# One sum of all experts in 32 slot columns, and the first block's rows from four partial sums

## The chip, the core and the metric

The kernel runs on one core of a Trainium2 chip. The metric is the device time of one execution in microseconds. Before the change its median over three runs is 196.35 us (196.34 to 196.45).

A core has these engines, each with its own instruction queue, worked off in order: TensorE (PE; its weight loads are shown apart as PEld), VectorE (DVE), ScalarE (ACT) and GpSimd (POOL). SyncE (SP) issues transfers here, and POOL issues those of the weights. Sixteen transfer engines move the data. SBUF holds 128 partitions; TensorE writes into PSUM, eight banks, from which VectorE and ScalarE copy results out. In a matmul one operand is loaded as weights (rows x columns) and the other streams through.

## What is computed

A gated recurrence runs over 4 sequences of 5056 tokens with 256 channels, and its output goes through a mixture of experts with 32 slots (8 experts with 4 slots each):

```python
f = lower_bound + (1 - lower_bound) * sigmoid(f_logit);  i = 1 - f
h[t] = f[t] * h[t-1] + i[t] * x[t]                 # per sequence and channel
logits = h @ phi                                   # 20224 x 32
d = softmax of logits over all tokens              # per slot
slot_input = d.T @ h                               # 32 x 256
slot_out[e] = relu(slot_input[e] @ w1[e]) @ w2[e]  # 8 experts, F = 1024
c = softmax of logits over the 32 slots            # per token
out = c @ slot_out                                 # 20224 x 256, f32
```

Every output row needs all of `slot_out`, and `slot_out` needs every token. So nothing of the output can leave before the experts are done.

## The kernel before

**First phase.** Groups of 512 tokens are loaded, gated, turned to channels, scanned by VectorE, turned back, and fed to the logits and to the slot sums. The exponentials of the logits stay in `etall` (bf16): 32 partitions for each of the four sequences, one column for each token. The weights come in by POOL's queue (`load_w`, L135): `w1` for eight experts, then `w2` for eight. The last two experts' `w2` lie in `w_t`, and the last of all is loaded in two issues, 6 and 2 of its 8 pieces (L144). All orders are written out by hand (`manual_schedule`), so each engine takes its work in the order of the code.

**Experts.** The slot inputs go through `w1`, four experts at a time (L661), and the rectified hidden values are transposed by TensorE (L674). The first four experts then use `hid`: for every expert and piece a weight block of 32 slot columns in which only the expert's own four are not zero. Piece `fc` works on column group `fc % 4`, so four groups of 32 PSUM partitions each hold a partial sum (L693). It is copied out as `so4` (L699). The other four experts use `wide`: the same columns repeated four times, once for each sequence, so 128 columns (L707). Between them one f32 matmul with `rep2`, a 128x128 pattern of 32x32 identities, adds the four partial sums of `so4` and repeats them (L711). So `so_ps` holds the complete `slot_out` four times, one below the other. Row sums of the weights (L413), a long f32 matmul without use for the result (`long_spin`, L156) and two more (`spin`, L152) stand between the experts.

**From slots to rows.** `slot_out` is cast to bf16 (L720). POOL multiplies it by two parity columns into `slot_bd` (L722), so that one matmul with 64 rows serves two sequences at once.

**Output.** `pieces` (L765) makes the first block of sequence 0, 16 rows for each partition, in steps of 2, 2, 2, 4 and 6 rows. Each row is a matmul of 32 partitions of `etall` with `slot_out` (`share`, L736), then ScalarE (first half of a step) and VectorE (second half) scale it by `rrow` into `ob_first`, and SP issues a transfer for each step (L777). Then `by_rows` (L780) makes the last, shorter block, two sequences at a time from `slot_bd` (L788), scaled by VectorE and ScalarE in turn (L730, L795) into `oc`, and sent by two transfers (L753). Then come `rest`, the other three sequences of the first block (`whole`, L808), and the middle block (`couple`, L819). The first stage takes its PSUM tiles by `first_op` from two banks of `psu` and six of `pfirst`.

Of the kernel before, what the change touches and what calls it, by code (L numbers as in the profile page):

```python
# [9 lines left out]
F32 = mybir.dt.float32  # L10
BF16 = mybir.dt.bfloat16
# [7 lines left out]
def kernel(  # L19
# [148 lines left out]
    with tc.tile_pool(name="sp2", bufs=3) as sp2, \  # L168
# [332 lines left out]
        for n in range(n_unit):  # L501
# [94 lines left out]
            elif not n >= n_unit - 6:  # L596
# [2 lines left out]
                batch(slots, n - 4, 1)  # L599
                if n > 2 * B and n % (2 * B) == 3:  # L600
                    idle(1)
        hid, wide = (ld.tile([P, 2, R, D], F32, name=i, tag="x_t") for i in ("hid", "wide"))
        hid = hid.rearrange("p u r d -> p (u r d)").bitcast(BF16)[:, ds(0, FC * E // 2 * NS)]
        wide = wide.rearrange("p u r d -> p (u r d)").bitcast(BF16)[:, ds(0, FC * E // 2 * P)]
        nc.gpsimd.memset(hid, 0.0)
        nc.gpsimd.memset(wide, 0.0)
        hid = hid.rearrange("p (f e s) -> p f e s", f=FC, s=NS)
        wide = wide.rearrange("p (f w b s) -> p f w b s", f=FC, b=B, s=NS)
        logits(last, [3])
        late_exps()  # L610
        left_over()
# [24 lines left out]
    ofirst = ctx.enter_context(tc.tile_pool(name="ofirst", bufs=1, side="right"))  # L636
    ob_first = ofirst.tile([P, wide_r * D + 120], F32, name="ob_first")
    ob_first = ob_first[:, ds(0, wide_r * D)].rearrange("p (r d) -> p r d", d=D)

    with tc.tile_pool(name="ew", bufs=1) as ew, \  # L640
         tc.tile_pool(name="pm", bufs=2, space=PSUM) as pm, \
         tc.tile_pool(name="pbig", bufs=1, space=PSUM) as pbig:

        rep2 = rep.rearrange("p b s -> p (b s)")

        sin = ew.tile([P, DC, NS], BF16, name="sin")
        for o in range(DC):
            nc.vector.scalar_tensor_tensor(sin[:, o], sin_ps[:, o], omlb[:, ds(o, 1)], rcs,
                                           ALU.mult, ALU.mult)

        Q = 4
        H = F // 2
        his = []
        for q in range(E // Q):
            hi = ew.tile([P, F], BF16, name=f"hi{q}")
            for k in range(2):
                hi_ps = (psu.tile([P, H], F32, name="hi_ps", tag="up") if q == 0 else
                         pbig.tile([P, H], F32, name="hi_ps", tag=f"hi_ps{k}"))
                for o in range(DC):
                    for j in range(Q):  # L660
                        nc.tensor.matmul(hi_ps[ds(j * NS, NS)], sin[:, o],  # L661
                                         w1_sb[q * Q + j][:, o, ds(k * H, H)],
                                         start=(o == 0), stop=(o == DC - 1),
                                         skip_group_check=True)
                if k == 0:
                    nc.scalar.activation(hi[:, ds(k * H, H)], hi_ps, ACT.Relu)
                else:
                    nc.vector.tensor_scalar_max(hi[:, ds(k * H, H)], hi_ps, 0.0)
            his.append(hi)
        for q in range(E // Q):  # L670
            ht_ps = psu.tile([P, FC, P], BF16, name="ht_ps", tag="up")
            hi_v = his[q].rearrange("p (c f) -> p f c", f=FC)
            for fc in range(FC):
                nc.tensor.transpose(ht_ps[:, fc], hi_v[:, fc], ident)  # L674
            if q == 0:
                src = ht_ps.rearrange("p f (j s) -> p f j s", s=NS)[:, :, :, ds(0, SPE)]
                src = bass.AP(tensor=src.tensor, offset=src.offset,
                              ap=[list(src.ap[0]), [P, FC], [NS + SPE, Q], [1, SPE]])
                dst = hid[:, :, :, ds(0, SPE)]
                dst = bass.AP(tensor=dst.tensor, offset=dst.offset,  # L680
                              ap=[list(dst.ap[0]), [Q * NS, FC], [NS + SPE, Q], [1, SPE]])
                nc.scalar.copy(dst, src)
                continue
            for j in range(Q):
                s0 = (Q + j) * SPE
                src = ht_ps[:, :, ds(j * NS + s0, SPE)]
                copy = nc.scalar.copy if j % 2 == 0 else nc.vector.tensor_copy
                copy(wide[:, :, j, :, ds(s0, SPE)],
                     src.unsqueeze(2).broadcast_to([P, FC, B, SPE]))
        so4_ps = pm.tile([P, D], F32, name="so4_ps", tag="pm")  # L690
        for e in range(Q):
            for fc in range(FC):
                nc.tensor.matmul(so4_ps[ds(fc % 4 * NS, NS), :], hid[:, fc, e],  # L693
                                 w2_sb[e][:, fc],
                                 start=(e == 0 and fc < 4),
                                 stop=(e == Q - 1 and fc >= FC - 4),
                                 skip_group_check=True)
        so4 = ew.tile([P, D], F32, name="so4")
        nc.vector.tensor_copy(so4, so4_ps)  # L699
        so_ps = pm.tile([P, D], F32, name="so_ps", tag="pm")  # L700
        row_sums(1, range(4, 16))
        nc.vector.reciprocal(rrow[:, :wide_r], rs_ps[:, :wide_r])
        for j in range(Q):
            if j == 2:
                long_spin(tail[:, 1], 3)
            for fc in range(FC):
                nc.tensor.matmul(so_ps, wide[:, fc, j].rearrange("p b s -> p (b s)"),  # L707
                                 w2_sb[Q + j][:, fc], start=j == 0 and fc == 0,
                                 stop=j == Q - 1 and fc == FC - 1, skip_group_check=True)
            if j == 0:  # L710
                nc.tensor.matmul(so_ps, rep2, so4, start=False, stop=False,  # L711
                                 skip_group_check=True)
                row_sums(2)
            if j == 1:
                q = n_grp * R - 1
                nc.vector.reciprocal(rrow[:, wide_r:q], rs_ps[:, wide_r:q])
                nc.vector.reciprocal(rrow[:, q, ds(0, B // 2)], rs_ps[:, q, ds(0, B // 2)])
        ops = [psu.tile([P, 2, D], F32, name="op", tag="up")]
        spin(ops[0].rearrange("p u d -> p (u d)"), 2, G)
        nc.vector.tensor_copy(slot_out, so_ps)  # L720
        for u in range(2):
            nc.gpsimd.tensor_scalar_mul(slot_bd[:, u], slot_out, parity[:, ds(u, 1)])  # L722


    held.close()
# [1 line left out]
    with tc.tile_pool(name="osb", bufs=3) as osb:  # L727
# [37 lines left out]
        def pieces(i, b):  # L765
            dst = rows_of(i, b)
            ob = ob_first
            r0 = 0
            for k in (1, 1, 1, 2, 3):
                for j in range(2):  # L770
                    for r in range(r0 + j * k, r0 + j * k + k, 2):
                        n = min(2, r0 + j * k + k - r)
                        op = first_op()
                        share(op, i, b, r, n)
                        (by_scalar, by_vector)[j](ob[:, ds(r, n)], op[:, ds(0, n)],
                                                  scale_of(i, b, r, n))
                nc.sync.dma_start(out=dst[:, ds(r0, 2 * k)], in_=ob[:, ds(r0, 2 * k)])  # L777
                r0 += 2 * k

        def by_rows(i, j):  # L780
            t0, n_r = blocks[i]
# [119 lines left out]
```

## Time and profile before

| | |
|---|---|
| median of three runs | 196.35 us |
| the profiled execution's own time | 196.46 us |
| its span on the core | 194.7 us |
| PE busy | 148.0 us (76%) |
| VectorE busy | 142.1 us (73%) |
| ScalarE busy | 138.4 us (71%) |
| POOL busy | 102.5 us (53%) |
| read from HBM, written to it | 58.23 MB, 20.71 MB |

The span is the time between the first and the last instruction that the profiler recorded; all positions below are microseconds from its start. A row of a view of instructions reads: start, length, engine, line of the code, operation, output tile <- input tiles, shape; a group has its number of instructions behind an x, and its length is that from the first's start to the last's end. In brackets stand the idle time of the engine before it and what ended that. A window's row has for each engine its busy time and the number of instructions, then the clock that TensorE was granted (1.00 is full), the share of the transfer engines that was busy, and GB/s. "DMA to landing" is the time from the start of an issue until the data are in place.

### The profile page before, as it was taken

What the parts mean: (1) busy time and instruction counts of PE and PEld (TensorE: products, weight loads), DVE (VectorE), ACT (ScalarE), POOL (GpSimd) and SP (SyncE); (2) the same over time, 40 slices, a digit from 0 to 9 for tenths busy, and PEclk for the clock granted to TensorE, in tenths of its full rate; (3) what the DMA queues carried; (4) which work ended last, traced back from release to release, by engine and by line L of the source; (5) the groups of instructions that cost most, each with busy time, mean ns of one, the idle gap of its engine ahead of it and who ended that gap; (6) DMA issues with size and microseconds to landing.
All of it is one profiled execution on the core that took longest, in us unless ns stands there. A gap on an engine that the chain in (4) does not pass through costs nothing.

```text
span 194.7 us, 3260 instructions
## 1 busy us (share of the span) xinstructions
PE 148.0 (76%) x1216; PEld 105.2 (54%) x1216; DVE 142.1 (73%) x176; ACT 138.4 (71%) x192; POOL 102.5 (53%) x77
## 2 busy tenths in 40 slices
PE   0685686997989979898898976999696999980000
PEld 0474555685767758666685765667461764420000
DVE  2666899899799999999999999443178767770000
ACT  3687889799789998899998697421068688992000
POOL 2586877874998688884979977580030000000000
PEclk9999999699999999999999999999996555555555
DMA  5999999999999999999999999999939999999995
GB/s 200 418 434 423 428 428 421 431 431 356 373 426 426 405 338 423 426 428 344 391 412 398 269 221 213 214 215 214 177 149 425 432 447 431 431 431 431 431 431 222
DMA packets 11953, 70.75 MB, mean 363 GB/s; under 512 B 1297, under 2 KB 1682, under 8 KB 7458
## 3 DMA queue, kind: packets, MB, share of 16 engines
q1 hardware_dynamic: 9456, 62.13, 76.4%
q0 software_dynamic: 2480, 8.42, 21.6%
q8 instruction: 9, 0.15, 0.3%
q14 instruction: 6, 0.05, 0.1%
q10 hardware_dynamic: 2, 0.00, 0.0%
HBM read 58.23 MB, written 20.71 MB: 406 GB/s over the span
## 4 chain that ended last, share of the span: by engine, by line
PE 31%; DVE 23%; DMA 19%; ACT 6%; POOL 6%; issue 4%; SPq 1%; POOLq 1%; ACTq 0%; DVEq 0%
DVE h L334 16%; DMA w_t<-in_moe_w_dram 10%; PE op L829 7%; DMA w_sb<-in_moe_w_dram 6%; PE op L740 5%; POOL u_t L247 5%; PE hp L347 4%; PE up L266 4%; PE sp L251 4%; DMA f_t<-in_f_logit_dram 4%; DVE ht L366 3%; ACT s_t L236 3%; DVE oc L730 2%; PE lg L380 2%; PE slot_ps L185 1%
## 5 line engine op out<-in xcount | busy, mean ns | idle before, releaser
L247 POOL TENSOR_TENSOR u_t<-s_t,x_t 128x1024 bf16<-128x1024 bf16 (+1 forms) x39 | 82.3, 2127 | 21.7 <-ACT s_t L236 14.8
L334 DVE TENSOR_TENSOR_SCAN h<-a,h,up 128x512 bf16<-128x512 f32 x64 | 78.1, 1266 | 5.5 <-PE up L266 2.8
L236 ACT ACTIVATE s_t<-f_t 128x2048 bf16<-128x2048 f32 (+2 forms) x23 | 38.2, 1669 | 5.9 <-DMA f_t<-in_f_logit_dram 5.7
L347 PE MATMUL hp<-ident_f,h 128*128 128x128 f32 (+1 forms) x160 | 29.1, 305 | 7.4 <-DVE ht L366 4.7
L347 PEld LDWEIGHTS hp<-ident_f,h 128*128 128x128 f32 (+1 forms) x160 | 23.1, 206 | 16.4 <-DVE ht L366 9.3
L299 ACT ACTIVATE a<-sp,lbs 128x1024 f32<-128x1024 bf16 x28 | 29.7, 1114 | 2.2 <-PE sp L251 2.2
L251 PE MATMUL sp<-ident_f,s_t 128*128 128x128 f32 x144 | 21.4, 292 | 7.1 <-ACT s_t L236 5.7
L266 PE MATMUL up<-ident_f,u_t 64*128 64x64 f32 x224 | 21.2, 233 | 4.2 <-POOL u_t L247 4.0
L251 PEld LDWEIGHTS sp<-ident_f,s_t 128*128 128x128 f32 x144 | 17.4, 150 | 8.8 <-ACT s_t L236 6.7
L266 PEld LDWEIGHTS up<-ident_f,u_t 64*128 64x128 f32 x224 | 16.7, 141 | 8.9 <-POOL u_t L247 5.0
L366 ACT COPY ht<-hp 128x512 f32<-128x512 f32 (+1 forms) x21 | 12.2, 582 | 4.8 <-PE hp L347 4.8
L306 ACT ACTIVATE a<-sp,lbs 128x512 f32<-128x512 bf16 (+2 forms) x16 | 13.2, 867 | 2.6 <-PE sp L251 2.4
L185 PE MATMUL slot_ps<-rep,ident_f 128*128 128x256 f32 x42 | 13.8, 419 | 0.0
L366 DVE COPY ht<-hp 128x512 f32<-128x512 f32 (+1 forms) x19 | 12.7, 668 | 0.8 <-PE hp L347 0.8
L829 PE MATMUL op<-slot_bd,etall 64*128 64x512 bf16 x32 | 13.1, 626 | 0.0
L840 ACT ACTIVATE oc<-op,rrow 128x256 f32<-128x256 f32 x32 | 12.2, 486 | 0.8 <-PE op L829 0.3
L740 PE MATMUL op<-slot_out,etall 32*128 32x256 bf16 x64 | 12.6, 374 | 0.1
L834 DVE TENSOR_TENSOR oc<-op,rrow 128x1024 f32<-128x1024 f32 x8 | 9.7, 1223 | 3.3 <-PE op L829 3.3
L740 PEld LDWEIGHTS <-etall 32*128 32x128 bf16 x64 | 9.0, 153 | 3.9 <-issue 1.7
L734 ACT ACTIVATE ob<-op,rrow 128x256 f32<-128x256 f32 x24 | 9.4, 474 | 2.1 <-PE op L740 1.7
L380 PE MATMUL lg<-h,phi 128*32 128x512 bf16 (+1 forms) x80 | 10.5, 405 | 0.2 <-ACT et L404 0.2
L334 DVE TENSOR_TENSOR_SCAN h<-a,up 128x512 bf16<-128x512 f32 x8 | 9.3, 1208 | 1.6 <-PE up L251 0.9
(110 smaller groups left out, 170.0 us busy)
## 6 DMA issues: line engine op xcount, KB each, us to landing
f_t<-in_f_logit_dram SPq DMA_DIRECT2D x14, 1024.0 KB, 12.4
x_t<-in_x_dram SPq DMA_DIRECT2D x14, 1024.0 KB, 11.4
w_sb<-in_moe_w_dram POOLq DMA_DIRECT2D x14, 512.0 KB, 10.9
out_dram<-ob SPq DMA_DIRECT2D x3, 2048.0 KB, 9.7
f_t<-in_f_logit_dram SPq DMA_DIRECT2D x8, 512.0 KB, 8.6
x_t<-in_x_dram SPq DMA_DIRECT2D x8, 512.0 KB, 7.7
out_dram<-oc SPq DMA_DIRECT2D x1, 4096.0 KB, 13.9
out_dram<-oc SPq DMA_DIRECT2D x2, 2048.0 KB, 15.3
```

What stands on the lines that cost most here:

```text
L185: nc.tensor.matmul(slot_bank[:, 1], ident_f, wide_rep, start=first, stop=False, skip_group_check=True)
L236: nc.scalar.activation(s_t, f_t, ACT.Sigmoid, scale=-1.0)
L247: nc.gpsimd.tensor_tensor(uts[n][:, :r], s_t[:, :r], x_t[:, :r], ALU.mult)
L251: nc.tensor.transpose(ps[:, :, r], t[:, r].bitcast(F32), ident_f)
L266: nc.tensor.transpose(v[:, :, r], t(r)[k].bitcast(F32), ident_f[k, k])
L299: nc.scalar.activation(a, sp[:, :, :, :, o], ACT.Identity, scale=nomlb[:, ds(o, 1)], bias=1.0)
L334: nc.vector.tensor_tensor_scan(h[:, :T, o], decays[n // 2, o][:, n % 2, :T], up[:, :T, o], hs[number(g - 1, b)][:, ds(used(g - 1) - 1, 1), ...
L347: nc.tensor.transpose(hp[:n_p, r], hw[:, :n_p, r], ident_f)
L366: copy(hts[g][:n_p, b].rearrange("p r d -> p (r d)").bitcast(F32), hps.pop(n)[:n_p].rearrange("p r c -> p (r c)"))
L380: nc.tensor.matmul(lg[ds(b * NS, NS), :], phi[:, o], hs[number(g, b)][:, :T, o], start=o == 0, stop=o == DC - 1, skip_group_check=True)
L740: nc.tensor.matmul(op[:, j], ew[:, :, r + j], slot_out[ds(b * NS, NS)], start=True, stop=True, skip_group_check=True)
L829: nc.tensor.matmul(op[:, i_r].rearrange("p u d -> p (u d)"), ew[:, :, r + i_r], slot_bd[ds(j * 2 * NS, 2 * NS)].rearrange("s u d -> s (u d)"),
```

## The change

All eight experts now use `hid`, which is twice as large, and the column groups; `wide` and `so4` are gone. `so_ps` then holds four partial sums, not the complete result four times. Three things follow from that:

- `parts` is the bf16 cast of the partial sums. The first block's rows are computed from it: a row's weights for sequence 0 (32 partitions of `etall`) are repeated to 128 partitions in `four`, so that the matmul over 128 rows adds the four partial sums itself. `four` is made between the experts by four matmuls with `copies` (the pattern `rep2` cut to 32 rows, in bf16) and four copies out of PSUM.
- `total` is the f32 copy of the same sums. The matmul with `rep2` that adds and repeats them now stands inside `pieces`, after the second step.
- `slot_out` and `slot_bd` are made from its result after the third step.

`long_spin` stands once more, before the last expert. An unused PSUM tile `aside` takes the place that `so4_ps` had.

```diff
@@ -599,13 +599,10 @@
                 batch(slots, n - 4, 1)
                 if n > 2 * B and n % (2 * B) == 3:
                     idle(1)
-        hid, wide = (ld.tile([P, 2, R, D], F32, name=i, tag="x_t") for i in ("hid", "wide"))
-        hid = hid.rearrange("p u r d -> p (u r d)").bitcast(BF16)[:, ds(0, FC * E // 2 * NS)]
-        wide = wide.rearrange("p u r d -> p (u r d)").bitcast(BF16)[:, ds(0, FC * E // 2 * P)]
+        hid = ld.tile([P, 2, R, D], F32, name="hid", tag="x_t")
+        hid = hid.rearrange("p u r d -> p (u r d)").bitcast(BF16)[:, ds(0, FC * E * NS)]
         nc.gpsimd.memset(hid, 0.0)
-        nc.gpsimd.memset(wide, 0.0)
-        hid = hid.rearrange("p (f e s) -> p f e s", f=FC, s=NS)
-        wide = wide.rearrange("p (f w b s) -> p f w b s", f=FC, b=B, s=NS)
+        hid = hid.rearrange("p (q f e s) -> p q f e s", q=2, f=FC, s=NS)
         logits(last, [3])
         late_exps()
         left_over()
@@ -636,6 +633,11 @@
     ofirst = ctx.enter_context(tc.tile_pool(name="ofirst", bufs=1, side="right"))
     ob_first = ofirst.tile([P, wide_r * D + 120], F32, name="ob_first")
     ob_first = ob_first[:, ds(0, wide_r * D)].rearrange("p (r d) -> p r d", d=D)
+    four = ofirst.tile([P, P * wide_r], BF16, name="four")
+    parts = ofirst.tile([P, D], BF16, name="parts")
+    total = ofirst.tile([P, D], F32, name="total")
+    copies = ofirst.tile([P, P], BF16, name="copies")
+    nc.gpsimd.tensor_copy(copies[ds(0, NS)], rep[ds(0, NS)].rearrange("p b s -> p (b s)"))
 
     with tc.tile_pool(name="ew", bufs=1) as ew, \
          tc.tile_pool(name="pm", bufs=2, space=PSUM) as pm, \
@@ -672,54 +674,58 @@
             hi_v = his[q].rearrange("p (c f) -> p f c", f=FC)
             for fc in range(FC):
                 nc.tensor.transpose(ht_ps[:, fc], hi_v[:, fc], ident)
-            if q == 0:
-                src = ht_ps.rearrange("p f (j s) -> p f j s", s=NS)[:, :, :, ds(0, SPE)]
-                src = bass.AP(tensor=src.tensor, offset=src.offset,
-                              ap=[list(src.ap[0]), [P, FC], [NS + SPE, Q], [1, SPE]])
-                dst = hid[:, :, :, ds(0, SPE)]
-                dst = bass.AP(tensor=dst.tensor, offset=dst.offset,
-                              ap=[list(dst.ap[0]), [Q * NS, FC], [NS + SPE, Q], [1, SPE]])
-                nc.scalar.copy(dst, src)
-                continue
-            for j in range(Q):
-                s0 = (Q + j) * SPE
-                src = ht_ps[:, :, ds(j * NS + s0, SPE)]
-                copy = nc.scalar.copy if j % 2 == 0 else nc.vector.tensor_copy
-                copy(wide[:, :, j, :, ds(s0, SPE)],
-                     src.unsqueeze(2).broadcast_to([P, FC, B, SPE]))
-        so4_ps = pm.tile([P, D], F32, name="so4_ps", tag="pm")
-        for e in range(Q):
+            own = ht_ps.rearrange("p f (j s) -> p f j s", s=NS)[:, :, :, ds(q * Q * SPE, SPE)]
+            own = bass.AP(tensor=own.tensor, offset=own.offset,
+                          ap=[list(own.ap[0]), [P, FC], [NS + SPE, Q], [1, SPE]])
+            dst = hid[:, q, :, :, ds(q * Q * SPE, SPE)]
+            dst = bass.AP(tensor=dst.tensor, offset=dst.offset,
+                          ap=[list(dst.ap[0]), [Q * NS, FC], [NS + SPE, Q], [1, SPE]])
+            nc.scalar.copy(dst, own)
+
+        def fourfold(i):
+            ps = psu.tile([P, G], F32, name="four_ps", tag="up")
+            nc.tensor.matmul(ps, copies[ds(0, NS)],
+                             etall[ds(0, NS), ds(i * G, G)], start=True, stop=True,
+                             skip_group_check=True)
+            copy = nc.scalar.copy if i % 2 == 0 else nc.vector.tensor_copy
+            copy(four[:, ds(i * G, G)], ps)
+
+        aside = pm.tile([P, D], F32, name="aside", tag="pm")
+        nc.vector.memset(aside[:, ds(0, 1)], 0.0)
+        so_ps = pm.tile([P, D], F32, name="so_ps", tag="pm")
+
+        def expert(e):
             for fc in range(FC):
-                nc.tensor.matmul(so4_ps[ds(fc % 4 * NS, NS), :], hid[:, fc, e],
+                nc.tensor.matmul(so_ps[ds(fc % 4 * NS, NS), :], hid[:, e // Q, fc, e % Q],
                                  w2_sb[e][:, fc],
                                  start=(e == 0 and fc < 4),
-                                 stop=(e == Q - 1 and fc >= FC - 4),
+                                 stop=(e == E - 1 and fc >= FC - 4),
                                  skip_group_check=True)
-        so4 = ew.tile([P, D], F32, name="so4")
-        nc.vector.tensor_copy(so4, so4_ps)
-        so_ps = pm.tile([P, D], F32, name="so_ps", tag="pm")
+
+        for e in range(Q):
+            expert(e)
         row_sums(1, range(4, 16))
         nc.vector.reciprocal(rrow[:, :wide_r], rs_ps[:, :wide_r])
-        for j in range(Q):
-            if j == 2:
+        for e in range(Q, E):
+            if e == E - 2:
                 long_spin(tail[:, 1], 3)
-            for fc in range(FC):
-                nc.tensor.matmul(so_ps, wide[:, fc, j].rearrange("p b s -> p (b s)"),
-                                 w2_sb[Q + j][:, fc], start=j == 0 and fc == 0,
-                                 stop=j == Q - 1 and fc == FC - 1, skip_group_check=True)
-            if j == 0:
-                nc.tensor.matmul(so_ps, rep2, so4, start=False, stop=False,
-                                 skip_group_check=True)
+            expert(e)
+            if e == Q:
                 row_sums(2)
-            if j == 1:
+                fourfold(0)
+                fourfold(1)
+            if e == Q + 1:
                 q = n_grp * R - 1
                 nc.vector.reciprocal(rrow[:, wide_r:q], rs_ps[:, wide_r:q])
                 nc.vector.reciprocal(rrow[:, q, ds(0, B // 2)], rs_ps[:, q, ds(0, B // 2)])
+                fourfold(2)
+                fourfold(3)
+            if e == E - 2:
+                long_spin(tail[:, 1], 3)
         ops = [psu.tile([P, 2, D], F32, name="op", tag="up")]
         spin(ops[0].rearrange("p u d -> p (u d)"), 2, G)
-        nc.vector.tensor_copy(slot_out, so_ps)
-        for u in range(2):
-            nc.gpsimd.tensor_scalar_mul(slot_bd[:, u], slot_out, parity[:, ds(u, 1)])
+        nc.vector.tensor_copy(parts, so_ps)
+        nc.vector.tensor_copy(total, so_ps)
 
 
     held.close()
@@ -765,17 +771,28 @@
         def pieces(i, b):
             dst = rows_of(i, b)
             ob = ob_first
+            lanes = four.rearrange("s (p r) -> s p r", r=wide_r)
             r0 = 0
-            for k in (1, 1, 1, 2, 3):
+            for step, k in enumerate((1, 1, 1, 2, 3)):
                 for j in range(2):
                     for r in range(r0 + j * k, r0 + j * k + k, 2):
                         n = min(2, r0 + j * k + k - r)
                         op = first_op()
-                        share(op, i, b, r, n)
+                        for m in range(n):
+                            nc.tensor.matmul(op[:, m], lanes[:, :, r + m], parts,
+                                             start=True, stop=True, skip_group_check=True)
                         (by_scalar, by_vector)[j](ob[:, ds(r, n)], op[:, ds(0, n)],
                                                   scale_of(i, b, r, n))
                 nc.sync.dma_start(out=dst[:, ds(r0, 2 * k)], in_=ob[:, ds(r0, 2 * k)])
                 r0 += 2 * k
+                if step == 1:
+                    sum_ps = first_op()[:, 0]
+                    nc.tensor.matmul(sum_ps, rep2, total, start=True, stop=True,
+                                     skip_group_check=True)
+                if step == 2:
+                    nc.vector.tensor_copy(slot_out, sum_ps)
+                    for u in range(2):
+                        nc.gpsimd.tensor_scalar_mul(slot_bd[:, u], slot_out, parity[:, ds(u, 1)])
 
         def by_rows(i, j):
             t0, n_r = blocks[i]
```

## The prediction

> **What bounds the kernel now.** I read four things in this order: the page's slices, to see which resource is full when; the chain that ended last, over the hand-over from the first phase to the output; that stretch instruction by instruction; and the transfer rate in half-microsecond windows.
>
> The page's slices (each 4.87 us), rows for clock and transfers:
> ```profile
> PEclk9999999699999999999999999999996555555555
> DMA  5999999999999999999999999999939999999995
> GB/s 200 418 434 423 428 428 421 431 431 356 373 426 426 405 338 423 426 428 344 391 412 398 269 221 213 214 215 214 177 149 425 432 447 431 431 431 431 431 431 222
> ```
> The transfer engines are full in every slice but slice 30 (141.1 to 146.0 us). Before it the expert weights come in at about 214 GB/s, after it the 20.71 MB of output leave at 425 to 447. From 176 us on no engine computes, yet transfers run to the end. So compute late in the kernel costs nothing; what counts is when the last weights land, how soon the first output leaves, and whether the output queue then ever runs dry.
>
> The chain of waits, at the hand-over (start, length, what):
> ```profile
> 122.05 18.77 DMA w_t<-in_moe_w_dram
> 140.82 0.04 issue
> 140.86 1.10 PE so_ps L707 x8
> ...
> 141.99 0.43 DVE slot_out L720
> ...
> 143.51 0.91 POOL slot_bd L722
> 144.43 0.04 issue
> 144.47 0.60 PE op L788 x2
> ```
> The last expert starts when its first 6 of 8 weight pieces land (140.82). The other two are an issue of their own, with its landing time in the answer for that tile from 124 to 126 us (issue started at 124.56 in the timeline):
> ```profile
> L147 POOL DMA_DIRECT2D w_t<-in_moe_w_dram x1: 528/528/528, 124.6 to 124.6; - x1
> DMA to landing us min/median/max: 17.0/17.0/17.0
> ```
> 124.56 + 17.0 = 141.56. In narrow windows the eight matmuls of L707 start at 140.86, .97, 141.08, .19, .30, .41, then .57 and .68: the seventh waited for that landing. So only the last two matmuls lie behind the last weights, not all eight.
>
> The timeline of the hand-over:
> ```profile
> 141.79 0.59 PE L152 MATMUL op<-w_sb 128*128 128x512 bf16 x2
> 142.47 1.90 PE L740 MATMUL op<-slot_out,etall 32*128 32x256 bf16 x16
> 142.59 1.83 POOL L722 TENSOR_SCALAR slot_bd<-slot_out,parity 128x256 bf16<-128x256 bf16 x2 [12.00 <-DVE slot_out L720]
> 142.77 3.02 ACT L734 ACTIVATE ob_first<-op,rrow 128x256 f32<-128x256 f32 x8 [9.80 <-PE op L740]
> 142.88 2.61 DVE L730 TENSOR_TENSOR ob_first<-op,rrow 128x256 f32<-128x256 f32 x6 [0.47 <-PE op L740]
> 143.36 2.79 SPq L777 DMA_DIRECT2D out_dram<-ob_first  x5
> 145.41 3.07 DVE L730 TENSOR_TENSOR oc<-op,rrow 128x512 f32<-128x512 f32 x5
> 145.63 3.07 ACT L795 ACTIVATE oc<-op,rrow 128x256 f32<-128x256 f32 x8
> 148.05 0.39 SPq L753 DMA_DIRECT2D out_dram<-oc  x1
> ```
> `slot_bd` is ready at 144.42, while VectorE and ScalarE work on the first block's rows until 145.4 and 145.6: about 1.0 us of cover. The second kind of output (`oc`, 1792 KB) is issued at 148.05.
>
> The windows (last column GB/s):
> ```profile
> 144.00:144.50 0.50, 0.40 (x5) 0.29 (x4) 0.50 (x2) 0.50 (x2) 0.42 (x1) 1.00 0.57 221
> 148.50:149.00 0.50, 0.50 (x2) 0.00 (x0) 0.50 (x2) 0.50 (x3) 0.00 (x0) 0.50 0.97 406
> 149.00:149.50 0.50, 0.03 (x1) 0.00 (x0) 0.50 (x2) 0.50 (x3) 0.00 (x0) 0.50 1.02 424
> ```
> First bytes leave at about 144.24 (half of a full window), 0.88 after the issue at 143.36. Added up window by window, the 2.10 MB of the first five transfers are out at 149.24. The next is issued at 148.05, so its data are ready at 148.93: only 0.31 us before the queue would run dry. That is the tightest place that the change touches.
>
> **The change part by part.** I sum against the profiled execution: 196.46 us, span 194.7; the median is 196.35, 0.11 less. About 0.2% (0.39 us) is what a measurement here can tell from no change.
>
> *Preparation, under the weight transfers.* POOL issues every weight load (the last at 124.56) before the memsets, so moving those shifts no load. There it sheds a memset of 3.53, the other grows from 0.97 to about 1.9, and one 32x128 copy comes in (rows of L86: 0.28); its copies for L416 are done earlier. ScalarE and VectorE lose the `wide` copies (0.27 and 0.22 each) and `so4` (0.42), and gain two copies each of 128x512 (rows of L666 and L668: 0.60 and 0.69). TensorE loses the f32 replication between experts (0.60) and gains four matmuls and a second long spin (0.81). The third and fourth fourfold copies end at about 138.1; PE's long spin waits for the reciprocals behind VectorE's first copy, about 137.3, and ends near 138.3. Expert 6's weights land at 139.0, so 0.7 us hides it. The second spin runs 139.3 to 140.1, against 140.82. Price: nothing.
>
> *Experts on column groups.* 32 matmuls of L693 take 1.06 us, 0.033 apart, against 0.109 for L707. The last expert needs 8 x 0.033 instead of 8 x 0.109, which looks like 0.6 us. But matmuls 7 and 8 still wait for 141.56: they start at 141.57 and 141.60 and end at 141.88 (0.27 long) instead of 141.95. The gain is 0.08, not 0.6.
>
> *The first transfer.* `parts` takes VectorE 0.42 as `slot_out` did: 141.91 to 142.34; the first row matmul at 142.39 (was 142.47). A 128-row weight load (L413, 0.148) costs about what a 32-row one (L740, 0.138) does. `total` follows `parts`, until about 142.69, and VectorE's first row product starts at 142.80, when its matmul is ready anyway. First issue at 143.28: −0.08.
>
> *The sum moved behind two steps.* Each step: matmuls of steps 0 and 1 at 142.39, 142.50, 142.75 (its bank may have to wait for `total`), 142.86. Then the f32 sum: two passes, 0.44 apart from the next (L711: 135.03 to 135.47), 142.97 to 143.41; result at about 143.57. Step 2's matmuls at 143.41 and 143.52; VectorE's product 143.82 to 144.23; only then, in VectorE's order, `slot_out`: 144.16 to 144.58 (starts of such operations lie 0.34 apart). POOL 0.17 later, 1.83 long: `slot_bd` at 146.59, 2.17 later than now. POOL has nothing else queued and SP's order is unchanged; what waits is PE (L805), behind which VectorE, ScalarE and the `oc` transfers wait.
>
> VectorE's remaining row products start at 144.50, 145.10, 145.70 and end at 146.11, so the fourth and fifth transfers go at about 145.24 and 146.17 (now 144.78 and 145.82). Their data follow the third's end within 0.1 us; the first block still leaves at 149.25.
>
> With `slot_bd` at 146.59 the block matmul runs at 146.64 and VectorE starts its rows at 147.04 instead of 145.41: 1.63 later, the 1.0 us cover gone. Same pace (four at 0.60, ScalarE six at 0.36; the half clock of the last rows adds 0.1 to 0.2): the `oc` issue comes at 149.75 instead of 148.05, its data at 150.6.
>
> *The pause.* Seen from the mean of the transfer engines, the queue is dry from 149.25 to 150.6: +1.36. Seen from the slowest it is less: the last piece landed 145.82 + 4.6 = 150.4, and this `oc` transfer 148.05 + 6.6 = 154.65. On an idle queue 256 KB landed in 2.0; 1536 KB more at 430 GB/s add 3.66, so issued at 149.75 it lands at 155.41: +0.76. Both ends come from rows; nothing says which engines set the end, so I take the middle, **+1.05**. Later transfers have cover: the second `oc` is issued near 152.6 (its predecessor flows to 154.9), the next full block at about 158.4 (needed by 159.7 less 0.88). The first transfer's −0.08 is already in these times.
>
> One rule speaks against even that 0.08. The Trainium skill (TensorEngine Tiling, Key Properties) says that a change of tiling mode, not merely of tile, drains TensorE. The trace agrees: between L693 (128*32) and L413 (128*128) starts lie 0.20 apart, not 0.03. By the rule the spin after the last expert starts at 141.88, the first row matmul at 142.47, and the sum is +1.13 instead of +1.05.
>
> Sum: 196.46 + 1.05 = 197.5 profiled; from the median, **197.4**.
>
> **Rivals.**
> *No pause.* If `slot_bd` came 1.3 us sooner, or the first block drained that much slower, the new start would hide: −0.08, so 196.3. For it: the slowest engines still carry the first block until about 150. Against it: POOL's 0.92 per product, twice, and VectorE's fixed order.
>
> *The clock falls.* The profile's clock is 0.50 from 34.8 to 38.2 us and from 147.5 on, although PE was recorded busy for 3.02 of the 3.41 us from 144.06 to 147.47, with 32- and 64-row matmuls. The change cuts PE's expert work from 1.03 to 0.27 per expert (four times) and adds only 0.81 of full-array spin. If that pulls the clock down over 141 to 147.5, L740's spacing doubles (0.119 to 0.222), the sum takes 0.88, `slot_bd` comes near 147.85, PE then feeds rows 0.43 apart, and the `oc` issue goes to about 151.95: landing 157.6, +2.9, 199.3. A fall over a part of it gives 198.2. Against it: both spins still come just before. The Trainium skill (TensorE: Matmul & The Clock Gate, What's actually happening) says that the clock halves after at least one idle window of about 3.4 us; PE never pauses that long, so by that rule this rival gets no chance. The trace disagrees with it, by the 3.02 busy microseconds.
>
> *Faster, by lagging transfer engines catching up.* The fifth transfer landed at 150.4, though the mean was through at 149.24 and landing follows data by some 0.5: its slowest engine lags 0.65. In a full queue such a lag stays to the end; a short pause lets it close. With a pause on the mean under 0.3 us the end comes up to 0.6 sooner: 195.8. It decides if `oc` is issued before about 148.6, so `slot_bd` by 145.5. I find no path to that.
>
> **How the numbers follow.** Forecast (a pause of 0.5 to 1.5): 0.60, own range 196.8 to 197.9. No pause to speak of: 0.13. Clock: 0.15. Catching up: 0.12. The range 196.0 to 198.7 leaves out most of the third's upper part and most of the last case. Faster 0.12, same 0.13, slower 0.75 (forecast and clock).
>
> **What would show it.** Right: the last expert's seventh matmul waits for a landing near 141.6; the first output issue moves by under 0.15; `slot_bd` ends near 146.6; the first `oc` issue is near 149.75; the windows from 149 to 151 show a dip of 0.8 to 1.4 us in all, and none before. Wrong: full windows there; or `slot_bd` before 145.5; or a granted clock of 0.5 before 147; or weights that land well before or after 141.6.

## The result

The changed kernel takes 198.46 us (median of 4, 198.23 to 198.59), the kernel before beside it 196.40: 2.06 us more, ratio 1.010 with a 95% interval of 1.0085 to 1.0115. The profiled execution took 198.59, 2.13 more than that of before (196.46).

The slices of the changed kernel (each 4.92 us), rows for clock and transfers:
```profile
PEclk9999999699999999999999999999589655555555
DMA  5999999999999999999999999999556999999996
GB/s 203 420 428 428 426 425 430 428 426 343 390 433 426 386 348 421 433 421 321 413 418 361 262 216 213 213 214 211 112 228 290 423 446 426 423 426 426 430 426 266
```
Besides the first and the last slice, three instead of one now have transfer engines that are not full (numbers 29 to 31, 137.8 to 152.5 us), and the clock is at half in a slice where it had been full.

Rows of the timeline of the hand-over in the changed kernel (others between them are left out):
```profile
139.71 1.65 PE L156 MATMUL tail<-rep,ident_f 128*128 128x384 f32 x2
141.29 0.62 PE L699 MATMUL so_ps<-w_t,hid 128*32 128x256 bf16 x8
141.84 1.03 PE L152 MATMUL op<-w_sb 128*128 128x512 bf16 x2
141.97 0.42 DVE L727 CAST parts<-so_ps 128x256 bf16<-128x256 f32 x1 [3.58 <-PE so_ps L699]
142.67 1.06 PE L782 MATMUL op<-parts,four 128*128 128x256 bf16 x4
143.52 0.78 PE L790 MATMUL op<-total,rep 128*128 128x256 f32 x2
143.83 3.41 SPq L786 DMA_DIRECT2D out_dram<-ob_first  x5
144.90 0.41 DVE L793 CAST slot_out<-op 128x256 bf16<-128x256 f32 x1
145.50 1.83 POOL L795 TENSOR_SCALAR slot_bd<-slot_out,parity 128x256 bf16<-128x256 bf16 x2 [17.21 <-DVE slot_out L793]
147.38 1.67 PE L805 MATMUL op<-slot_bd,etall 64*128 64x512 bf16 x8 [1.76 <-POOL slot_bd L795]
147.84 4.88 DVE L736 TENSOR_TENSOR oc<-op,rrow 128x512 f32<-128x512 f32 x8 [1.00 <-issue]
148.33 4.48 ACT L812 ACTIVATE oc<-op,rrow 128x256 f32<-128x256 f32 x12 [1.58 <-issue]
150.69 2.52 SPq L759 DMA_DIRECT2D out_dram<-oc  x2
```
The last expert's eight matmuls are short, as meant, but the result is copied at 141.97, where it had been 141.99. The spin behind them takes 1.03 instead of 0.59, so the first row's matmul starts at 142.67 (was 142.47), and the first output is issued at 143.83 (was 143.36). `slot_bd` is ready at 147.33 (was 144.42) and the first `oc` transfer goes at 150.69 (was 148.05).

The windows of the changed kernel (the last three columns: granted clock, share of the transfer engines, GB/s):
```profile
144.50:145.00 0.50, 0.50 (x7) 0.50 (x6) 0.44 (x2) 0.50 (x2) 0.00 (x0) 1.00 0.62 242
...
146.50:147.00 0.50, 0.00 (x0) 0.00 (x0) 0.34 (x2) 0.25 (x1) 0.50 (x1) 1.00 0.75 299
...
149.50:150.00 0.50, 0.50 (x4) 0.24 (x3) 0.50 (x2) 0.50 (x3) 0.00 (x0) 1.00 0.73 295
150.00:150.50 0.50, 0.50 (x3) 0.20 (x2) 0.50 (x2) 0.50 (x3) 0.00 (x0) 1.00 0.05 16
150.50:151.00 0.50, 0.36 (x2) 0.00 (x0) 0.50 (x2) 0.50 (x3) 0.00 (x0) 1.00 0.00 0
151.00:151.50 0.50, 0.05 (x1) 0.00 (x0) 0.50 (x2) 0.50 (x2) 0.00 (x0) 1.00 0.00 0
```
From these rows the loss can be added up; windows with a share of 0.87 or more count as full, since the kernel before has such dips too (down to 0.94). The first bytes leave 0.62 x 0.5 us before 145.00, at 144.69; in the kernel before, 0.57 x 0.5 before 144.50, at 144.22. That is 0.47 later. After that the queue is short of work by 0.13 (146.5), 0.14, 0.48, 0.50 and 0.50: 1.74 us; before, by nothing. Together 2.21, against 2.13 measured.

Why the clock fell: the windows of the changed kernel, cut where the granted clock changes.
```profile
133.65:137.06 3.41, 2.32 (x33) 1.30 (x30) 1.91 (x4) 0.58 (x1) 0.00 (x0) 1.00 1.07 214
137.06:140.47 3.41, 3.41 (x13) 1.14 (x12) 0.69 (x1) 0.58 (x1) 0.00 (x0) 0.50 0.98 187
140.47:143.89 3.42, 3.42 (x17) 1.58 (x16) 1.25 (x4) 0.75 (x2) 0.00 (x0) 0.50 0.10 18
143.89:147.30 3.41, 1.73 (x14) 1.51 (x13) 2.64 (x6) 2.49 (x7) 1.80 (x2) 1.00 0.76 296
```
PE (first busy column) had 2.32 us of work in the window before the fall, with the experts on column groups and the 32-row fourfold matmuls; then the clock is at half for two windows, which take in the stretch from the last weights (141.5) to the start of the sum (143.5).

### The profile page after: what moved, and what is told of

The parts are those of the page before. It is cut to its first block, busy times and chain, and to the rows that moved or that the text cites. A ratio compares the mean times of both kernels' runs of the same rounds, so it can differ in the third digit from the quotient of the medians.

```text
span 196.8 us, 3275 instructions
## 1 busy us (share of the span) xinstructions
PE 148.7 (76%) x1222; PEld 103.9 (53%) x1222; DVE 143.5 (73%) x178; ACT 139.5 (71%) x193; POOL 100.3 (51%) x77
## 4 chain that ended last, share of the span: by engine, by line
PE 35%; DVE 22%; DMA 10%; ACT 9%; POOL 8%; issue 6%; POOLq 1%; ACTq 0%; DVEq 0%
DVE h L334 14%; DMA w_sb<-in_moe_w_dram 9%; PE op L846 7%; POOL u_t L247 6%; PE op L746 5%; PE sp L251 5%; PE hp L347 4%; PE up L266 4%; DVE ht L366 3%; ACT s_t L236 3%; DVE h L321 3%; ACT oc L812 2%; DMA f_t<-in_f_logit_dram 2%; PE lg L380 2%; PE tail L156 2%
## 5 line engine op out<-in xcount | busy, mean ns | idle before, releaser
L795 POOL TENSOR_SCALAR slot_bd<-slot_out,parity 128x256 bf16<-128x256 bf16 x2 | 1.8, 918 | 17.2 <-DVE slot_out L793 17.2
L746 PE MATMUL op<-slot_out,etall 32*128 32x256 bf16 x48 | 9.8, 385 | 0.0
```

Of the source, the lines that this page charges most:

```text
L746: nc.tensor.matmul(op[:, j], ew[:, :, r + j], slot_out[ds(b * NS, NS)], start=True, stop=True, skip_group_check=True)
```

## The experiments

Two theories stood against each other. Q, the output queue: the time follows from when the first transfer starts and how long the queue is dry afterwards; the clock matters by what it does to these two. C: the fallen clock is the whole loss. All diffs are against the changed kernel unless it says otherwise.

**Two more f32 matmuls, to hold the clock (a_warm).**
```diff
                 fourfold(0)
                 fourfold(1)
+                long_spin(aside, 2)
+                long_spin(aside, 2)
```


> The changed kernel with two more f32 matmuls of 128x256 on the full array (about 0.86 us, into an unused PSUM tile) between the fifth and sixth expert. Theory Q (output queue): the change costs what the first output transfer starts later plus how long the queue then runs dry before the first oc transfer; the half clock from 137.1 to 143.9 us is only the cause of the first part. Q with the clock kept at full: first transfer issued near 143.3 instead of 143.83, slot_bd ready near 146.6 instead of 147.33, oc issued near 149.8 instead of 150.69, 197.5 to 197.8 us. Theory C (clock alone): the half clock is the whole loss; then about 196.4. If the extra matmuls do not keep the clock up, the time stays at 198.4.

Measured 197.93 (197.75 to 198.00), ratio to the kernel before 1.0071 (1.0056 to 1.0086). The clock was full from 51 us until 153. Rows of its timeline:
```profile
142.39 0.78 PE L784 MATMUL op<-parts,four 128*128 128x256 bf16 x4 [0.19 <-DVE parts L729]
143.29 3.24 SPq L788 DMA_DIRECT2D out_dram<-ob_first  x5
144.80 1.83 POOL L797 TENSOR_SCALAR slot_bd<-slot_out,parity 128x256 bf16<-128x256 bf16 x2 [15.88 <-DVE slot_out L795]
147.15 3.68 DVE L738 TENSOR_TENSOR oc<-op,rrow 128x512 f32<-128x512 f32 x6 [1.01 <-issue]
147.63 3.39 ACT L814 ACTIVATE oc<-op,rrow 128x256 f32<-128x256 f32 x9 [1.59 <-issue]
150.00 0.39 SPq L761 DMA_DIRECT2D out_dram<-oc  x1
```
Its windows around the dry stretch:
```profile
149.00:149.50 0.50, 0.50 (x4) 0.24 (x3) 0.50 (x2) 0.50 (x3) 0.00 (x0) 1.00 0.47 184
149.50:150.00 0.50, 0.36 (x3) 0.09 (x1) 0.50 (x2) 0.50 (x3) 0.00 (x0) 1.00 0.04 16
150.00:150.50 0.50, 0.35 (x1) 0.00 (x0) 0.50 (x2) 0.50 (x3) 0.00 (x0) 1.00 0.00 0
150.50:151.00 0.50, 0.00 (x0) 0.00 (x0) 0.50 (x2) 0.50 (x3) 0.00 (x0) 1.00 0.41 172
```
With the clock full the first output starts as early as before the change, and 1.54 us of dry queue remain (0.27, 0.48, 0.50, 0.30). C falls: with the clock full 1.44 of the 2.06 us remain (197.93 against 196.49 beside it), so the clock was worth 0.5 to 0.6. The time lies just above the upper end of what Q expected, since `oc` went at 150.00, not 149.8.

A second profile of it (a_warm_2) says the same: full clock from 38.6 to 147.8, first output issued at 143.30, `oc` at 150.01, 1.61 us of dry queue, 197.94.

> The kernel with two more f32 matmuls between the fifth and sixth expert once more. If these hold the clock: full clock from 130 to 147 again, first transfer issued near 143.3, the queue dry for 1.5 to 1.6 us, 197.7 to 198.0. If the first profile was a lucky position: half clock before 144 and 198.4.

**Half of slot_bd on ScalarE (c_split).**
```diff
                 if step == 2:
                     nc.vector.tensor_copy(slot_out, sum_ps)
-                    for u in range(2):
-                        nc.gpsimd.tensor_scalar_mul(slot_bd[:, u], slot_out, parity[:, ds(u, 1)])
+                    nc.gpsimd.tensor_scalar_mul(slot_bd[:, 0], slot_out, parity[:, ds(0, 1)])
+                if step == 3:
+                    nc.scalar.activation(slot_bd[:, 1], slot_out, ACT.Copy, scale=parity[:, ds(1, 1)])
```


> The changed kernel, with the second half of slot_bd made by ScalarE (after its products of the fourth step) instead of POOL. The first output transfer and the clock stay as they are. Q: slot_bd is ready near 146.4 instead of 147.33, oc issued near 149.8 instead of 150.69, the dry stretch 0.9 us shorter, 197.5 to 197.7. C: no change, 198.4.

Median 196.96 of 10, spread from 196.59 to 198.15; ratio 1.0034 (1.0016 to 1.0052). `slot_bd` was ready at 146.26, `oc` issued at 149.36, and the dry stretch shrank to 0.46. The direction is Q's, but the gain is larger than Q expected: 1.28 us less dry queue instead of 0.9, and 1.50 us in the time. One part is in the trace: ScalarE, which now has work until then, starts its first `oc` row 0.26 behind VectorE (146.99 and 146.73), where it was 0.49 in the changed kernel (148.33 and 147.84). The start did not stay as expected either: the profiled execution had the clock full, and still issued its first output at 143.85. There the first phase ended late: the experts began at 134.85 instead of 131.95, PE no longer waited for weights, and the second long spin stood in front of the last expert until 142.01, with the first six pieces of its weights landed at 141.1.

A second profile (c_split_2) was later still: the last weights' load was issued at 127.52 (124.54 in the first profile), the experts began at 136.05, and the time was 199.65, far from the 196.6 to 197.3 expected.

> The kernel with half of slot_bd on ScalarE once more, as its times spread from 196.6 to 198.2. Start of the first transfer and dry stretch decide: with the clock at half before 144, issue near 143.8 and a pause of 0.4 to 0.7, 196.9 to 197.3; with full clock, issue near 143.3 and 196.6.

What makes the first phase of these executions late was not settled; both had the clock at half for over 10 us of it in one stretch (35.9 to 46.1, and 33.8 to 47.5), where the kernel before and the changed one had it so for 3.4. The edit does not touch that phase.

**The wait alone, in the kernel before (d_delay).** Two more POOL products that nothing reads; against the kernel before:
```diff
         nc.vector.tensor_copy(slot_out, so_ps)
+        for u in range(2):
+            nc.gpsimd.tensor_scalar_mul(extra[:, u], slot_out, parity[:, ds(u, 1)])
         for u in range(2):
             nc.gpsimd.tensor_scalar_mul(slot_bd[:, u], slot_out, parity[:, ds(u, 1)])
```


> The kernel before, with two more POOL products of the same size (1.83 us, into a tile that nothing reads) ahead of those for slot_bd; nothing else is changed. It prices the wait by itself at full clock. Q: slot_bd 146.25 instead of 144.42, oc issued near 149.35 instead of 148.05, its data at 150.2 where the queue has run dry at 149.24: 0.8 to 1.0 us, so 197.2 to 197.4. If the slowest transfer engines set the end: +0.4, 196.8. C: no change, 196.4.

Median 198.13 of 5 (197.53 to 199.64), ratio 1.0087 (1.005 to 1.0123). The first output was issued at 143.32, as before, and `slot_bd` was ready at 146.17, as computed. But `oc` went at 150.23, not 149.35. Rows of the timeline of this kernel show why:
```profile
146.23 4.55 PE L791 MATMUL op<-slot_bd,etall 64*128 64x512 bf16 x13 [1.90 <-POOL slot_bd L725]
146.85 0.69 DVE L733 TENSOR_TENSOR oc<-op,rrow 128x512 f32<-128x512 f32 x1 [1.40 <-PE op L791]
147.60 3.39 ACT L798 ACTIVATE oc<-op,rrow 128x256 f32<-128x256 f32 x9 [1.85 <-issue]
147.70 0.69 DVE L733 TENSOR_TENSOR oc<-op,rrow 128x512 f32<-128x512 f32 x1 [0.16 <-PE op L791]
```
The clock was at half from 144.86 on; VectorE's rows come 0.85 apart instead of 0.60, each waiting for PE. The queue was dry for 1.83 us and the time rose by 1.64. So a wait for `slot_bd` alone, with nothing of the rest of the change, makes the queue run dry. Its price at full clock, which was the aim, was not measured: 0.88 of the 1.83 us is the `oc` issue at 150.23 instead of the expected 149.35, which came with the half clock. The rest, 0.95, is an estimate of that price, within Q's 0.8 to 1.0.

**Column groups without the fourfold weights (e_groups).** The sum, the cast and `slot_bd` stand ahead of the first row:
```diff
-        nc.vector.tensor_copy(parts, so_ps)
         nc.vector.tensor_copy(total, so_ps)
+        nc.tensor.matmul(aside, rep2, total, start=True, stop=True, skip_group_check=True)
+        nc.vector.tensor_copy(slot_out, aside)
+        for u in range(2):
+            nc.gpsimd.tensor_scalar_mul(slot_bd[:, u], slot_out, parity[:, ds(u, 1)])
...
-                        for m in range(n):
-                            nc.tensor.matmul(op[:, m], lanes[:, :, r + m], parts,
-                                             start=True, stop=True, skip_group_check=True)
+                        share(op, i, b, r, n)
```


> The changed kernel without the fourfold weights: all eight experts on column groups, then the f32 sum, the cast and slot_bd before the first row, which uses 32 partitions as in the kernel before. Q: the f32 copy (0.42), the sum (0.44 and 0.3 until its result) stand ahead of the first transfer at full clock: issue near 144.5, no dry stretch, 197.4 to 197.7; with the clock at half, the sum 0.8 and slower rows, 198.0 to 198.4. C: the clock falls here too, as the experts' work is as short: the same 198.4 as the changed kernel.

Median 198.71 (197.69 to 199.62), ratio 1.0115 (1.0069 to 1.0162). The clock was at half from 137.3 to 144.1, as in the changed kernel, the sum took 1.06 and the first output was issued at 145.35. The queue was never dry: the whole loss lies in the start, 1.99 us by the windows, 1.97 measured in the profiled execution (198.43). The median lies above both cases of Q, and C expected much the same, so this run does not separate the two theories. It shows the other way to pay for column groups: at half clock, the sum ahead of the first row costs about what the changed kernel loses in all (1.97 against 2.13). At full clock it was not measured.

**Both remedies (f_both).** The edits of a_warm and c_split together.

> The changed kernel with both remedies: the two extra f32 matmuls between the experts (clock) and the second half of slot_bd on ScalarE after the fourth step. Q: first transfer issued near 143.3, slot_bd ready near 145.7, oc issued near 148.85, its data at 149.7 where the queue is dry from 149.25: a pause of 0.4 instead of 1.6, so 196.8 to 196.95. If the pause were not what remains after the clock is kept: 197.9, as with the extra matmuls alone.

Median 196.77 (196.65 to 196.84), ratio 1.0013 (1.0004 to 1.0022). Its windows:
```profile
149.00:149.50 0.50, 0.27 (x1) 0.00 (x0) 0.50 (x2) 0.50 (x3) 0.00 (x0) 1.00 0.57 234
149.50:150.00 0.50, 0.00 (x0) 0.00 (x0) 0.50 (x2) 0.50 (x3) 0.00 (x0) 1.00 0.57 242
```
First output issued at 143.39, `oc` at 148.91, 0.43 us of dry queue. Only the edit of c_split lies between a_warm and this kernel: the dry time falls from 1.54 to 0.43 and the ratio from 1.0071 to 1.0013. With the clock full in both, this shows that the late `slot_bd` was the larger part of the loss. The two gains do not add up: c_split without the extra matmuls already had a median of 196.96.

**A further step (g_best).** f_both, with `total` copied by ScalarE and `slot_out` cast before VectorE's product of the third step:
```diff
-        nc.vector.tensor_copy(total, so_ps)
+        nc.scalar.copy(total, so_ps)
...
-                if step == 2:
                     nc.vector.tensor_copy(slot_out, sum_ps)
```


> As the kernel with both remedies, and moreover total is copied by ScalarE, which is idle there, and slot_out is cast before VectorE's product of the third step instead of after it. Q: slot_out ends near 143.9 instead of 144.6, VectorE reaches its first oc row near 145.8, oc issued near 148.5: a pause of about 0.1, 196.3 to 196.6, the same as the kernel before, since the earlier first transfer was worth 0.08 only. It would beat the kernel before by 0.5 or more only if column groups saved the 0.6 us that eight short matmuls seem to save.

Median 196.92 of 11 (196.63 to 199.29); ratio 1.0039 (1.0013 to 1.0066). No better than f_both: expected were 196.3 to 196.6. ScalarE did not copy `total` beside VectorE's `parts` but after it (142.71, `parts` from 142.19 to 142.62): its queue stands in a wait for VectorE's semaphore there, so the program itself puts the two readers of the PSUM tile one after the other, and the sum came no sooner. Its windows still lack 0.36 us in one place, and the weights landed 0.3 later in the profiled execution. Two rows of its timeline show what sets the last expert:
```profile
141.18 0.40 PE L699 MATMUL so_ps<-w_t,hid 128*32 128x256 bf16 x6 [0.17 <-DMA w_t<-in_moe_w_dram]
141.87 0.29 PE L699 MATMUL so_ps<-w_t,hid 128*32 128x256 bf16 x2 [0.30 <-DMA w_t<-in_moe_w_dram]
```
Six matmuls, a pause, and the last two when the last two pieces of weights have landed. None of the versions beats the kernel before.

**Without the second long spin (h_onespin).**
```diff
-            if e == E - 2:
-                long_spin(tail[:, 1], 3)
         ops = [psu.tile([P, 2, D], F32, name="op", tag="up")]
```


> The changed kernel without the second long spin (before the last expert). The clock has fallen at 137.1 in the profiled changed kernel and came back at 143.9 after a window that held 0.9 us of that spin. If the clock needs a full window of full-array work to come back, it now stays at half through the first rows and the sum: first transfer near 143.8, slot_bd near 147.5 to 147.9, rows at half pace, oc issued near 151.5, 198.9 to 199.5. If the spin only delays the last expert (it ended at 141.36, the weights landed at 141.46), the time stays at 198.4 or falls to 198.2.

Median 198.96 (198.79 to 199.14), ratio 1.0124 (1.0109 to 1.014). The clock fell at 138.9 and came back at 145.7, so it was at half through the first rows and the sum, as the first case had it: first output at 143.87, `slot_bd` ready at 147.86, `oc` issued at 151.24. The queue was dry in three places, 2.27 us in all. But it came back after two windows, as in the changed kernel with the spin; and after_2, the changed kernel once more (below), which has the spin, was slower still with its windows in almost the same position. So what the second spin is worth to the clock stays open. That it can stand in the way of the last expert shows in c_split.

**The changed kernel once more (after_2).**

> The changed kernel once more, for another position of the clock's windows. The clock rule: a window of 3.41 us with little full-array work between the experts brings the clock to half somewhere from 134 to 139 us for one or two windows, wherever the windows lie; first transfer issued later than 143.6. If the fall in the first profile was only an unlucky position: full clock until 147, issue near 143.3.

199.44. The clock was at half from 138.56 to 145.39, the first output went at 144.11, `slot_bd` was ready at 148.10, `oc` went at 151.54. So the fall was no accident of the first profile. The half clock covers later work than in the first profile, the sum and all rows until 145.39, and it comes again at 148.80, while the `oc` rows are made; the time is 0.85 longer.

**The accounts together.** For each profile, from half-microsecond windows as above: when the first bytes leave, compared with 144.22; the dry time after that; their sum; and the profiled execution's time less 196.46.

| kernel | start | dry | sum | measured |
|---|---|---|---|---|
| changed | +0.47 | 1.74 | 2.21 | 2.13 |
| after_2 | +0.75 | 2.25 | 3.00 | 2.98 |
| a_warm | −0.08 | 1.54 | 1.46 | 1.42 |
| a_warm_2 | −0.07 | 1.61 | 1.54 | 1.48 |
| c_split | +0.49 | 0.46 | 0.95 | 0.79 |
| c_split_2 | +2.86 | 0.38 | 3.24 | 3.19 |
| d_delay | −0.04 | 1.83 | 1.79 | 1.67 |
| e_groups | +1.99 | 0.00 | 1.99 | 1.97 |
| f_both | +0.02 | 0.43 | 0.45 | 0.38 |
| g_best | +0.23 | 0.36 | 0.59 | 0.50 |
| h_onespin | +0.50 | 2.27 | 2.77 | 2.68 |

The two terms give every one of the eleven times to within 0.16 us, and always a little too much. This says that no third term of size is at work; what made a start late or a queue dry it does not say, that rests on the pairs of kernels above. Q stands.

## Why the prediction was right, and where its sum was off

The direction and the cause were right: a dry output queue behind a `slot_bd` that comes too late. The size was half of what was measured (+1.05 against +2.06). About 0.4 of the difference is in the pause, by its length and by the `oc` issue behind it, as the kernel with a held clock shows (+1.44); the other 0.6 goes with the half clock. So the number was luckier than the sum: 198.46 lies outside the forecast's own range (196.8 to 197.9) and inside the wide one (196.0 to 198.7) only by the room made for the rival of the clock, and a later execution of the same kernel took 199.44. Of the signs, the seventh matmul (141.50) and a dip in the windows came as described, though the dip was longer than the 0.8 to 1.4 named; the first issue moved by 0.47, and the clock was at half before 147, which had been named as a sign of being wrong.

- **The last expert: right.** Column groups saved 0.09, not 0.6. Where the clock was full the path from the last weights' landing to the first issue shortened from 1.80 (141.56 to 143.36) to 1.71 in a_warm (124.58 + 17.0 = 141.58 to 143.29).
- **The first transfer, −0.08: wrong by 0.55.** It held with a full clock only: a_warm issued at 143.29, the forecast was 143.28. In the changed kernel it was 143.83. The prediction covered the shorter expert work by the second spin ("Price: nothing"); that cover failed. This was the rival "The clock falls", with a chance of 0.15. It came in part, from 137.06 to 143.89, near its lower price of 198.2; after_2 came near its upper one of 199.3.
- **The sum behind two steps: right at full clock.** `slot_bd` was forecast at 146.59; a_warm had 146.63. In the changed kernel the half clock added 0.74 to that.
- **The `oc` issue: 0.25 too early even at full clock** (149.75 against 150.00). VectorE's first row came at 147.15 (forecast 147.04), but ScalarE's only at 147.63, 0.48 behind instead of 0.22. The last of the waits for semaphores in ScalarE's queue ahead of that row begins at 145.07 and lasts 2.24, until 147.31, and the row starts 0.32 after it; what these 0.32 are, no run shows. In the kernel before, the same wait was 0.66 long and over while ScalarE was still busy.
- **The pause: mis-sized by the choice.** The prediction bounded it by +0.76 (slowest transfer engines) and +1.36 (their mean) and took the middle. In these runs the mean is nearer: in a_warm 1.54 us of missing windows cost 1.42. With the mean and the 0.25 above, 1.36 + 0.25 = 1.61, the time with a held clock would have been forecast at 198.0; a_warm has 197.93.
- **Preparation hidden by the weights: right** for VectorE, ScalarE and POOL. The second spin took 1.65 instead of 0.81 and held the last expert up from 140.8 to 141.29. That cost nothing, as the last two pieces landed at 141.5 only. In c_split it did cost: there the last expert began behind the spin at 142.01, with all its weights in place from 141.74.
- **Draining at a change of tiling:** beside its sum, the prediction gave 0.08 for it by the Trainium skill (TensorEngine Tiling, Key Properties). The trace of a_warm agrees with a delay, of 0.11: the spin starts 0.22 after the expert's last matmul (141.59 to 141.81), where it was 0.11 behind the 128-column matmuls of the kernel before (141.68 to 141.79). It cost nothing: the first row's matmul came at 142.39, where the sum without the rule had put it, as it waited for the cast of `parts`. The 0.20 against 0.03 of the prediction overstates it, since full-width matmuls follow each other at 0.11 anyway.
- **Faster, by transfer engines that catch up:** did not come; in no kernel with the change was `oc` issued before 148.9, and the shortest pause was 0.36. That lagging engines catch up in a pause is not shown; the at most 0.16 by which the accounts come out too high is all the room for it.

## What to carry to other kernels

Where a queue of transfers is the bound, write down for each issue when the queue would run dry and when the data will be ready, and subtract: here the spare time was 0.31 us, so a step that delayed one operand by 2.2 us left the queue dry for 1.5. Saving work behind a wait gains only what lies behind the last landing, 0.09 of an apparent 0.6 here. And when TensorE's work is cut, ask whether it was also what held its clock (by the share of the array that it fills, as the next section shows), and price the next stretch at half.

## What the runs showed of the hardware

- Busy time as recorded does not tell when the clock falls. It fell after windows with 2.32 us of PE work (changed kernel) and with 3.02 (kernel before), and not after one with 2.63 (kernel before) or with 1.64 (a_warm). The first two rows are from the kernel before, the third from a_warm; the clock fell behind the second alone:
```profile
133.82:137.23 3.41, 2.63 (x27) 2.19 (x25) 1.31 (x3) 0.00 (x0) 0.00 (x0) 1.00 1.06 213
144.06:147.47 3.41, 3.02 (x14) 1.41 (x13) 3.41 (x7) 3.41 (x11) 0.36 (x1) 1.00 1.01 398
143.40:146.81 3.41, 1.64 (x14) 1.49 (x13) 2.57 (x6) 2.53 (x7) 1.83 (x2) 1.00 0.81 317
```
  What separates them is how much of the 128x128 array the matmuls use. Count each matmul's time, up to the start of the next, only by its share of the array (rows x columns of its weights): the window of the changed kernel then has 1.14 us, the three above have 2.64, 1.44 and 1.58. In the twelve profiles 110 windows after 115 us begin at full clock. All 12 with at most 1.20 us by this count were followed by half clock, all 92 with 1.52 or more by full clock, and of the 6 from 1.43 to 1.50 four fell. Before 115 us the border is less sharp: falls come up to 1.83, none above. This is a pattern worked out from the records, not a tested rule.
- With two extra full-array matmuls the clock held between the experts in all four profiles (a_warm twice, f_both, g_best). Without them it fell there in four (the changed kernel twice, e_groups, h_onespin) and held in two (c_split twice), whose experts began late (134.85 and 136.05). A late start alone does not explain the four: in a_warm_2 and f_both the experts began at 132.57 and 132.62, within the 131.95 to 133.15 of those that fell. The Trainium skill (TensorE: Matmul & The Clock Gate, What's actually happening) tells of a fall after at least one idle window; here no window was idle.
- Coming back takes more than being busy: 137.06 to 140.47 was busy for all of its 3.41 us at half clock, and the clock stayed at half for another window.
- A kernel whose own stretch is unchanged can still take very different times by its first phase: executions of c_split ranged from 196.6 to 198.2, and one more took 199.65, with weights that landed 3 us later. Over the twelve profiles the experts begin the later, the longer the clock was at half in the first phase: at 131.95 to 132.28 with 3.4 us of it (four profiles; a fifth, g_best, at 133.36), 132.37 to 132.62 with 6.8 (three), 133.15 and 133.75 with 10.2, 134.85 with 13.7, 136.05 with 17.1. No run tests which of the two causes the other, so what triggers it stays open.
